# Layer-norm statistics and a check flag sent through DRAM, ScalarE copying all five sums, and a planner with other costs, latencies and due times

## The chip, the core and the metric

The kernel runs on one core of a Trainium2 chip. The metric is the device time of one execution in microseconds (us); lower is better. A time given for a kernel is the median of its runs. The core's engines each take their own queue of instructions in order: TensorE (PE) does the matmuls and transposes, VectorE (DVE) and ScalarE (ACT) the elementwise work, GpSimd (POOL) a few small operations and the DMAs that add into memory, SyncE (SP) issues most DMAs. An instruction waits where it stands until its semaphores allow it, and everything behind it on that engine waits too.

## The reference

One sequence of 2048 tokens with 640 features goes through a layer norm. A state-space convolution (S4D) and a two-layer network with the Mish activation both read the normalised input, and their results are added to the input.

```
xn = _layernorm(x)
...
dt = jnp.exp(log_dt)
A = -jnp.exp(log_A_real) + 1j * A_imag
C = (C_real + 1j * C_imag) * dt[:, None]
P = jnp.exp((A * dt[:, None])[:, :, None] * pos[None, None, :])
K = 2.0 * jnp.einsum("dn,dnl->dl", C, P).real
y = irfft(rfft(u_t, L2) * rfft(K, L2)[None], L2)[:, :, :L]
... y + u * D_skip
h = jnp.einsum("bsd,df->bsf", x, w1) + b1
act = h * jnp.tanh(softplus(h))
return jnp.einsum("bsf,fd->bsd", act, w2)
...
return x + _A_ref(xn, ...) + _B_ref(xn, ...)
```

The sizes are L = 2048, D = 640, N = 128 states for each feature and F = 1728 hidden units, all in float32.

## The kernel before

**Tiles.** Tokens go in four blocks of 512 (`TB`), features in five chunks of 128 (`KD`), hidden units in 14 chunks (`NF`): 13 of 128 and one of 64, chunk 8. Everything on chip is held transposed, features on partitions and tokens along the row. Each float32 operand of a matmul is split into a float16 hi part and a float16 lo part (what the hi part leaves), and a product is hi x hi + hi x lo + lo x hi. ACT makes the hi parts with a scaled copy, DVE the lo parts with one scalar_tensor_tensor: `hi_w1`/`lo_w1` and `hi_w2`/`lo_w2` for the weights, `hi0`/`lo0` for block 0 of the input and `hi_x`/`lo_x` for the others. Weights stay on chip once split.

**Network.** For every block and hidden chunk the first product (`mm1`, and `mm1_pair` for two chunks of the later blocks at once, in a form that needs fewer multiplications: parts one, two, three_a, three_b, four, with sums of weights and of inputs made ahead) fills a PSUM bank. Then a chain of ACT and DVE steps makes Mish: `sig` (sg), `mul` (v1), `mish_a1` to `mish_a3` (arctan, square, tanh), `mish_v3`, `mish_a4` (hi) and `mish_v4` (lo). The second product (`mm2_ops`, `mm2_last`) adds chunk after chunk into the five PSUM banks `ACC`, three chunks behind the first product (`LAG`). At the end of a block the five sums leave `ACC` by `join`: banks 0 and 1 by DVE, banks 2 to 4 by ACT. GpSimd's DMAs add the input to them, and `finish` and `store` add them to the block and store it.

**Recurrence.** The state-space part is done by two scans on DVE for each block and feature chunk (`skip_a` to `skip_e`), with coefficients worked out from the parameters (`mode_ops`). This form, and the scaling of the float16 splits, are right for parameters and weights within certain bounds. So the kernel measures them: `chk` squares and sums the weights, `chk_end` gives each partition a factor `ok`, `ok_sum` adds the 128 factors with a matmul by `ones`, `ok_end` makes a flag of the sum, and `load_flag` reads it into a register. A general form of the computation behind an If runs where the flag is set; with these inputs it isn't.

**Layer norm.** Block 0 is normalised at the start (`stat_ops`, `moments`, `norm0`, `norm0_a`), token by token, and then transposed by PE (`to_t0`) into `ACC`, from where ACT's `hi0` copies make `xh` and DVE's `lo0` make `xl`. For blocks 1 to 3 `stats` takes mean and variance of each token (DVE), `rstds` makes the pair (mean, 1/deviation) in a tile `st_row` of 128 x 8 (POOL), `spread` transposes that tile on PE into eight rows, `spread_a` copies the rows out of PSUM (ACT), `spread_d` writes them to DRAM, `spread_l` loads each row spread over all 128 partitions (`bc`), and `norm_t` applies them to the transposed input.

**What sets the order.** The program has two parts, each emitted under `tc.manual_schedule()`. The first, the start-up, is a string `ORDER`: S and M are statistics, N and A normalisation on DVE and ACT, T the transposes, H and L the hi and lo copies of a w1 chunk, h and l those of block 0's input (one feature chunk, one half of the tokens), and strings such as `0hhlh4a` products of the first three hidden chunks. Ahead of it stand the loads, all on SyncE's queue (half of the first two input tiles on ACT's):

```
for i in range(2):
    load_w1(i)
    sp.dma_start(X0[:, i + 2], xr[0, i + 2])
load_w1(2)
sp.dma_start(cv[:, 0:24], vec)
load_w1(3); load_w2(0); load_w1(4); load_w2(1); load_w1(5)
fill(13)
```

`fill` issues 13 small matmuls that warm PE up. The second part is all the rest, given as operations to a planner (`Plan`): `whole` adds each with its engine, a cost, what must be over before it (`pre`), the buffers that it takes and drops, and sometimes a due time; `run` simulates the engines with these costs, a gap behind each operation (`GAP`) and a latency behind each load, and emits the operations in the order in which that simulation starts them. PE's operations keep the order in which they are added. For the other engines the due time decides among those that could start: `dues` works it out backward from PE's order. The planner starts its engines at given times (`Plan({...})`), and takes the weights of the start-up as loaded: `("hw2", f)` for f = 0 and 1 and `("hw1", f)` for f = 4 and 5 have no load among what they wait for in the plan. These are ACT's hi copies of w2 chunks 0 and 1 and of w1 chunks 4 and 5. The real waits, on semaphores, are put in from the tiles that an instruction reads and writes.

Of the kernel before, what the change touches and what calls it, by code (L numbers as in the profile page):

```python
# [20 lines left out]
P = 128  # L21
# [37 lines left out]

class Plan:  # L60


    GAP = {"PE": 0.22, "ACT": 0.12, "DVE": 0.12, "SP": 0.0, "POOL": 0.3}
# [23 lines left out]
    def add(self, name, eng, cost, fn, pre=(), take=None, drop=(), due=None, rel=0.0, kb=0.0):  # L87
        assert name not in self.ops, name
        self.ops[name] = o = dict(name=name, eng=eng, cost=cost, fn=fn, pre=[p for p in pre if p not in self.end],
                                  take=take, drop=drop, due=1e9, soft=1e9 if due is None else due, rel=rel, kb=kb, n=len(self.ops))  # L90
        if eng == "PE":
            self.pe.append(o)
# [14 lines left out]
    def dues(self):  # L107
# [22 lines left out]
        for o in reversed(order):  # L130
            for p in o["pre"]:
                q = self.ops[p]
                if q["eng"] != "PE":
                    wait = 4.0 if q["kb"] else self.GAP[q["eng"]]
                    for u in ("due", "soft"):
                        q[u] = min(q[u], o[u] - o["cost"] - wait)

    def run(self):
        self.dues()
        todo = {e: {} for e in self.t}  # L140
# [3 lines left out]
        while any(todo.values()):  # L144
# [308 lines left out]
def body(ctx: ExitStack, tc: tile.TileContext, x, xT, logA, Aim, Cr, Ci, logdt, vec, w1, w1T, w2, w2T, out):  # L453
# [29 lines left out]
    ones = cst.tile([P, P], F32, name="ones")  # L483
    g.memset(ones, 1.0)
# [35 lines left out]
    pl = Plan({"PE": 20.05, "ACT": 15.5, "DVE": 17.0, "SP": 15.0, "POOL": 15.0})  # L520
# [115 lines left out]
    def spread():  # L636

        pe.transpose(TR[:2 * NT, 0:P], NX["st"].rearrange("p j i -> p (j i)"), ident)

    def spread_a():  # L640
        NX["sr"] = tmp.tile([2 * NT, P], F32, name="sr")
        a.copy(NX["sr"], TR[:2 * NT, 0:P])

    def spread_d():
        NX["sd"] = dram.tile([2 * NT, P], F32, name="sd")
        sp.dma_start(NX["sd"], NX["sr"])
# [17 lines left out]
    def mode_ops():  # L664
# [6 lines left out]
        yield "ACT", 3.4, lambda: a.activation(t()[:, 0], t()[:, 0], AF.Exp)  # L671
# [3 lines left out]
        for k in range(KD):  # L675
            yield "ACT", 0.5, lambda k=k: a.activation(t()[:, 2, k], t()[:, 2, k], AF.Copy, accum_out=sm[:, 0, k:k + 1])
# [53 lines left out]
    def ok_sum():  # L730
        pe.matmul(TR[:, 0:1], ones, SM["ok"], start=True, stop=True)
# [4 lines left out]
    def ok_end():  # L736
        v.tensor_scalar(flag, TR[0:1, 0:1], P - 0.5, None, op0=OP.is_lt)
# [27 lines left out]
    def join(b, k):  # L765
        r = pl["r", b, k]
        if k < 2:
            v.tensor_scalar(r, ACC[k], 1 / SO, None, op0=OP.mult)  # L768
        else:
            a.activation(r, ACC[k], AF.Copy, scale=1 / SO)  # L770
# [165 lines left out]
    def whole():  # L936
# [9 lines left out]
        def chain(b, f, pre, drop=()):  # L946
# [3 lines left out]
            if b > 0 and f in PAIRS:  # L950
                add(("sX", *n), A, 0.36, sig, b, f, PX, CA, pre=[("two", *n)], take=("s", ("s", *n), 2))
                add(("vX", *n), V, 0.38, mul, b, f, PX, CA, pre=[("sX", *n)], take=("A", ("A", *n), 1))
                add(("sg", *n), A, 0.36, sig, b, f, PZ, CB, pre=[("three_b", *n), ("sX", *n)])
                add(("v1", *n), V, 0.38, mul, b, f, PZ, CB, pre=[("sg", *n), ("vX", *n)], drop=[("s", *n)])
            else:
                add(("sg", *n), A, t(0.60, 0.36), sig, b, f, pre=pre, take=("s", ("s", *n), 2))
                add(("v1", *n), V, t(0.68, 0.38), mul, b, f, pre=[("sg", *n)], take=("A", ("A", *n), 1), drop=[("s", *n)])
            add(("a1", *n), A, t(0.63, 0.36), mish_a1, b, f, pre=[("sg", *n)], take=("p", ("p", *n), 1), drop=[("s", *n)])
            add(("a2", *n), A, t(0.63, 0.36), mish_a2, b, f, pre=[("a1", *n)])
            add(("a3", *n), A, t(0.63, 0.36), mish_a3, b, f, pre=[("a2", *n)])  # L960
            add(("v3", *n), V, t(0.61, 0.36), mish_v3, b, f, pre=[("a3", *n), ("v1", *n)], drop=[("p", *n)])
            add(("a4", *n), A, t(0.54, 1.44), mish_a4, b, f, pre=[("v3", *n)], take=("h", ("h", *n), 1))
            add(("v4", *n), V, t(0.62, 0.80), mish_v4, b, f, pre=[("a4", *n)], drop=[("A", *n)])
# [23 lines left out]
        for f in range(3):  # L987
            pl.end["m1", 0, f] = (16.7, 17.95, 20.1)[f]


        for f in range(NF):
            if f > 5:
                add(("lw1", f), S, 0.1, load_w1, f, take=("w", ("w1", f), 1), kb=327.0)
            if f > 3:
                add(("hw1", f), A, 0.65, hi_w1, f, pre=[("lw1", f)] if f > 5 else [])
                add(("ow1", f), V, 0.75, lo_w1, f, pre=[("hw1", f)], drop=[("w1", f)])
# [3 lines left out]
            add(("ow2", f), V, 0.75, lo_w2, f, pre=[("hw2", f)], drop=[("w2", f)])  # L1000
        for f in range(3):
            chain(0, f, [("m1", 0, f)])
        for f in range(3, NF):
# [4 lines left out]
            if f == 7:  # L1008
                add(("spread", 1), M, 0.1, spread, pre=[("rs", 1)])
# [7 lines left out]
        for b in range(1, NB):  # L1017
            for f in range(NF):
# [20 lines left out]
                lastA = [("v1", 0, 2), ("sr", 1)] if first else [("cY", *p0), ("vX", *p0)]  # L1039
                if (b, i) in ((1, 4), (2, 4), (3, 4)) and b < NB - 1:  # L1040
                    lastA.append(("sr", b + 1))
                if (b, i) == (NB - 1, NP - 1):
                    lastA.append(("oke",))
# [5 lines left out]
                add(("cV", *n), A, 0.36, lambda: a.copy(PVS, PV), pre=[("one", *n)] + ([] if first else [("w", *p0)]))  # L1049
                add(("cY", *n), A, 0.36, lambda: a.copy(PY, PX), pre=[("cV", *n), lastC])  # L1050
                A2[0]()
                add(("two", *n), M, 15 * M2, two, pre=[("cY", *n)] + SWD(1) + TXD(1) + XLD((1, 3, 4)))
                add(("z", *n), V, 0.38, lambda: v.tensor_tensor(PZ, PY, PVS, op=OP.add), pre=[("two", *n), lastB])
# [3 lines left out]
                add(("w", *n), V, 0.38, lambda: v.tensor_tensor(PW, PY, PVS, op=OP.add), pre=[("three_a", *n)])  # L1057
                add(("three_b", *n), M, 9 * M2, three_b, pre=[("z", *n)])
                if i == 3 and b < NB - 1:
                    add(("spread", b + 1), M, 0.1, spread, pre=[("rs", b + 1), ("vX", *n)])  # L1060
                if i == NP - 2 and b == NB - 1:
                    add(("oks",), M, 0.1, ok_sum, pre=[("ce", "last"), ("vX", *n)])
                    add(("oke",), V, 0.17, ok_end, pre=[("oks",)])
# [38 lines left out]
        for c in range(1, NB):  # L1102
            b = c - 1
            t0 = start(b, 0)
            for i in range(NT):
                add(("lx", c, i), S, 0.1, lambda c=c, i=i: sp.dma_start(pl["x", c, i], xr[c, i]),
                    pre=[("st", c, i - 2)] if i > 1 else [], take=("x", ("x", c, i), 1), rel=t0, kb=327.0)
                add(("st", c, i), V, 1.1, stats, c, i, pre=[("lx", c, i)] + [("st", c, i - 1)] * (i > 0), drop=[("x", c, i)])
            add(("rs", c), G, 2.6, rstds, pre=[("st", c, NT - 1)])
            add(("sr", c), A, 0.25, spread_a, pre=[("spread", c)])  # L1110
# [3 lines left out]
            add(("lxt", c), S, 0.5, load_xt, c, pre=old, rel=t0 + 10, kb=1310.0)  # L1114
# [233 lines left out]
```

## Time and profile before

| | |
|---|---|
| median of three runs | 357.91 us (357.82 to 358.10) |
| profiled execution, span of its trace | 356.0 us |
| VectorE busy | 305.9 us (86%) |
| ScalarE busy | 295.8 us (83%) |
| GpSimd busy | 48.9 us (14%) |
| moved by DMA | 48.75 MB, 137 GB/s on average |
| instructions | 6197 |

The profile is of one execution. Its page gives the busy time of each engine, the span in 40 slices, the DMA queues, the chain of work that ended last, and the costliest groups of instructions; the trace behind it tells each instruction's start and length. A row such as `7.86 1.21 ACT L1239 ACTIVATE xh<-acc 128x256 ... x4 [0.34 <-PE acc L1236]` reads: at 7.86 us from the span's start, over 1.21 us, ACT ran four instructions of line 1239 that read `acc` and write `xh`, and before them stood idle for 0.34 us, which the transposes of line 1236 on PE ended. `SPq` and `POOLq` are the queues on which SyncE and GpSimd issue DMAs. A helper's line covers all its calls, so operations are told apart by their tiles.

### The profile page before, as it was taken

Reading aid. Unit: us, or ns where it says so; the run is one execution under the profiler, and the core shown is the slowest. Engines: PE = TensorE matmul, PEld = TensorE weight load, DVE = VectorE, ACT = ScalarE, POOL = GpSimd, SP = SyncE. Lnnn points to the kernel's source line nnn. Section 1 sums busy time; section 2 is a strip of 40 time slices with the busy share of each in tenths; the row PEclk is TensorE's granted clock in tenths of the full one; section 3 lists DMA queues with packets and bytes.
Section 4 is the critical chain, followed back from the end, with each engine's and each line's share of the span. In section 5 each row is a group of like instructions: output and inputs, shape, how many; then the busy total and the mean of one; then the engine's idle time right before and its main releaser. Section 6 shows DMA issues by size and latency. Waiting matters only on the chain.

```text
span 356.0 us, 6197 instructions
## 1 busy us (share of the span) xinstructions
PE 350.0 (98%) x2257; PEld 215.1 (60%) x2257; DVE 305.9 (86%) x583; ACT 295.8 (83%) x620; POOL 48.9 (14%) x74
## 2 busy tenths in 40 slices
PE   7999999999999999999999999999999999999996
PEld 6754444444666666665566666566566666666543
DVE  5989989989999999999999877899988878895552
ACT  4699999987598699989899977989989979877650
POOL 2200010000014221000004341000002443000000
PEclk9999999999999999999999999999999999999999
DMA  7869964402819926910445982931000994032004
GB/s 266 327 175 288 321 217 121 142 0 66 287 56 159 295 71 142 347 40 3 130 151 88 252 204 77 309 120 40 28 0 7 164 216 102 18 58 32 2 2 152
DMA packets 26052, 48.75 MB, mean 137 GB/s; under 512 B 3592, under 2 KB 6944, under 8 KB 26016
## 3 DMA queue, kind: packets, MB, share of 16 engines
q1 hardware_dynamic: 19488, 34.86, 30.0%
q0 software_dynamic: 6240, 13.11, 18.5%
q8 instruction: 19, 0.31, 0.4%
q10 hardware_dynamic: 288, 0.33, 0.3%
q14 instruction: 17, 0.14, 0.2%
HBM read 39.10 MB, written 5.26 MB: 125 GB/s over the span
## 4 chain that ended last, share of the span: by engine, by line
PE 96%; DVE 1%; DMA 1%; ACT 0%; issue 0%
PE acc L859 48%; PE h L827 18%; PE h L807 12%; PE tr L827 12%; PE h L800 2%; PE h L789 2%; PE tr L789 1%; DMA x<-in_A_u_dram 1%; PE acc L1236 0%; DVE st L627 0%; DVE st L628 0%; ACT x L1224 0%; PE acc L873 0%; PE acc L871 0%; PE acc L870 0%; DVE w1l L556 0%
## 5 line engine op out<-in xcount | busy, mean ns | idle before, releaser
L859 PE MATMUL acc<-hi,w2h 128*128 128x512 f16 x273 | 100.9, 379 | 0.0
L859 PE MATMUL acc<-hi,w2l 128*128 128x512 f16 (+1 forms) x265 | 99.7, 379 | 0.0
L859 PE MATMUL acc<-lo,w2h 128*128 128x512 f16 x253 | 93.3, 379 | 0.0
L859 PEld LDWEIGHTS <-w2h 128*128 128x128 f16 x526 | 50.9, 98 | 48.3 <-issue 2.1
L890 ACT ACTIVATE s<-h,cv 128x512 f32<-128x512 f32 (+1 forms) x55 | 32.7, 595 | 28.6 <-PE h L827 23.4
L827 PEld LDWEIGHTS <-w1h 128*128 128x128 f16 x432 | 42.3, 98 | 10.7
L910 DVE SCALAR_TENSOR_TENSOR A<-p,A 128x512 f32<-128x512 f32 (+1 forms) x56 | 37.1, 662 | 8.5 <-ACT p L906 8.2
L859 PEld LDWEIGHTS <-w2l 128*128 128x128 f16 x273 | 25.6, 98 | 30.7 <-issue 1.1
L926 DVE SCALAR_TENSOR_TENSOR lo<-A,hi 128x512 f16<-128x512 f32 x52 | 35.5, 683 | 8.0 <-ACT hi L916 8.0
L894 DVE SCALAR_TENSOR_TENSOR A<-h,bs,s 128x512 f32<-128x512 f32 (+1 forms) x55 | 34.9, 637 | 6.2 <-ACT s L890 6.2
L898 ACT ACTIVATE p<-s,kc 128x512 f32<-128x512 f32 (+1 forms) x56 | 39.4, 703 | 0.6
L902 ACT ACTIVATE p<-p,kc 128x512 f32<-128x512 f32 (+1 forms) x56 | 39.4, 703 | 0.5
L906 ACT ACTIVATE p<-p,kc 128x512 f32<-128x512 f32 (+1 forms) x56 | 39.3, 702 | 0.4
L916 ACT ACTIVATE hi<-A 128x512 f16<-128x512 f32 x52 | 32.5, 626 | 2.6 <-DVE A L910 2.5
L548 POOL DMA_DIRECT2D r<-in_xT_dram x15 | 13.4, 1003 | 131.7 <-DVE r L768 66.3
L749 DVE TENSOR_TENSOR_SCAN g<-g,car,kc 128x512 f32<-128x512 f32 x20 | 25.6, 1278 | 1.7 <-ACT g L743 1.7
L827 PEld LDWEIGHTS <-w1l 128*128 128x128 f16 x216 | 21.1, 98 | 8.2
L753 DVE TENSOR_TENSOR_SCAN g<-g,car,g 128x512 f32<-128x512 f32 x20 | 25.5, 1276 | 0.0
L827 PE MATMUL tr<-xh,w1l 128*128 128x256 f16 x90 | 24.5, 273 | 0.0
L827 PE MATMUL tr<-xh,w1h 128*128 128x256 f16 x90 | 24.5, 273 | 0.0
L827 PE MATMUL tr<-xl,w1h 128*128 128x256 f16 x90 | 24.5, 273 | 0.0
L827 PEld LDWEIGHTS <-swh 128*128 128x128 f16 x216 | 21.1, 98 | 4.4
(177 smaller groups left out, 726.6 us busy)
## 6 DMA issues: line engine op xcount, KB each, us to landing
w<-in_w_dram SPq DMA_DIRECT2D x25, 320.0 KB, 4.9
x<-in_A_u_dram SPq DMA_DIRECT2D x14, 320.0 KB, 5.0
w<-in_w2T_dram SPq DMA_DIRECT2D x15, 288.0 KB, 6.4
w<-in_B_w_dram SPq DMA_DIRECT2D x13, 320.0 KB, 3.4
w<-in_w1T_dram SPq DMA_DIRECT2D x13, 320.0 KB, 7.0
xt<-in_xT_dram SPq DMA_DIRECT2D x15, 256.0 KB, 5.6
r<-in_xT_dram POOLq DMA_DIRECT2D x15, 256.0 KB, 5.6
xt<-r POOLq DMA_DIRECT2D x15, 256.0 KB, 4.6
```

The lines of the kernel that those rows point to most:

```text
L749: v.tensor_tensor_scan(g1[:, 1:], g1[:, 1:], zero.to_broadcast([P, TB]), car[:, 1, k:k + 1], op0=OP.add, op1=OP.add)
L807: pe.matmul(o, w, x, start=(j == 0), stop=(j == len(order) - 1))
L827: pe.matmul(o, p, q, start=start and n == 1, stop=n == 3 * len(w), skip_group_check=True)
L859: pe.matmul(o, w, x, start=start, stop=stop)
L890: a.activation(pl["s", b, f][:, c], bank(b, f)[:, c] if h is None else h, AF.Sigmoid, bias=cv[:, f:f + 1], scale=1 / SH)
L894: v.scalar_tensor_tensor(pl["A", b, f][:, c], bank(b, f)[:, c] if h is None else h, bs[:, f:f + 1], pl["s", b, f][:, c], op0=OP.add, op1=O ...
L898: a.activation(pl["p", b, f][:, cols(f)], pl["s", b, f][:, cols(f)], AF.Arctan, bias=one, scale=-1.0)
L902: a.activation(p, p, AF.Square, bias=pi4, scale=2.0)
L906: a.activation(p, p, AF.Tanh, bias=mb, scale=MG)
L910: v.scalar_tensor_tensor(A, pl["p", b, f][:, cols(f)], MC, A, op0=OP.add, op1=OP.mult)
L916: a.activation(hi, A, AF.Copy, scale=MA * SA / SH)
L926: v.scalar_tensor_tensor(lo, A, MA * SA / SH, hi, op0=OP.mult, op1=OP.subtract)
```

## The change

1. *Statistics.* `spread` and `spread_a` go. `spread_d` writes `st_row` straight to DRAM, turned by the access pattern of the DMA: 1024 single words of 4 bytes, where before eight rows of 512 bytes were written. `spread_l` is as before.
2. *Flag.* `ok_sum`, `ones` and the matmul go. `ok_row` writes the 128 factors to DRAM, `ok_back` loads them into one partition, and `ok_end` takes their minimum on DVE and makes the flag of it.
3. *Sums.* `join` has ACT copy all five banks of `ACC`.
4. *The planner's numbers.* Each operation gets the latency of its load as an argument (`lat`), PE's and ACT's gaps change, most costs change, the start times change by 0.3 to 0.35 us, and an operation can't be taken as ready before work of the start-up that it depends on.
5. *Due times.* A table `SHIFT` of 194 entries moves the due time of single operations, by their number in the plan, by -30 to 30 us, after `dues` has worked them out.

The first product's parts no longer wait in the plan for the copy of the rows (`sr`) or the flag's end (`oke`), since `TR` isn't used for them. The order of PE's operations in `whole` is the same, without the transposes and the ones. The core of the diff:

```
+SHIFT = [e.split(":") for e in (
+    "2:16.5 4:-11 5:-7.5 8:22.5 9:7.5 12:29 21:-23.5 27:12.5 28:-28 29:30 37:-23.5 39:5.5 40:22 41:19.5 45:16 "
...
+    "1335:-18.5 1336:-3.5 ").split()]
...
-    GAP = {"PE": 0.22, "ACT": 0.12, "DVE": 0.12, "SP": 0.0, "POOL": 0.3}
+    GAP = {"PE": 0.17, "ACT": 0.14, "DVE": 0.12, "SP": 0.0, "POOL": 0.3}
...
-    def add(self, name, eng, cost, fn, pre=(), take=None, drop=(), due=None, rel=0.0, kb=0.0):
+    def add(self, name, eng, cost, fn, pre=(), take=None, drop=(), due=None, rel=0.0, kb=0.0, lat=1.9):
         assert name not in self.ops, name
+        rel = max([rel] + [self.end[p] for p in pre if p in self.end])
...
-                    wait = 4.0 if q["kb"] else self.GAP[q["eng"]]
+                    wait = q["lat"] + 2.1 if q["kb"] else self.GAP[q["eng"]]
...
     def run(self):
         self.dues()
+        ops = list(self.ops.values())
+        for i, x in SHIFT:
+            for u in ("due", "soft"):
+                ops[int(i)][u] += float(x)
...
-                end = max(end, self.dma + 1.9)
+                end = max(end, self.dma + o["lat"])
...
-    pl = Plan({"PE": 20.05, "ACT": 15.5, "DVE": 17.0, "SP": 15.0, "POOL": 15.0})
+    pl = Plan({"PE": 20.4, "ACT": 15.8, "DVE": 17.3, "SP": 15.0, "POOL": 15.0})
...
-    def spread():
-
-        pe.transpose(TR[:2 * NT, 0:P], NX["st"].rearrange("p j i -> p (j i)"), ident)
-
-    def spread_a():
-        NX["sr"] = tmp.tile([2 * NT, P], F32, name="sr")
-        a.copy(NX["sr"], TR[:2 * NT, 0:P])
-
     def spread_d():
         NX["sd"] = dram.tile([2 * NT, P], F32, name="sd")
-        sp.dma_start(NX["sd"], NX["sr"])
+        sp.dma_start(NX["sd"].rearrange("r p -> p r"), NX["st"].rearrange("p j i -> p (j i)"))
...
-    def ok_sum():
-        pe.matmul(TR[:, 0:1], ones, SM["ok"], start=True, stop=True)
+    def ok_row():
+        NX["ok"] = tmp.tile([1, P], F32, name="ok_row")
+        z = dram.tile([P], F32, name="ok_dram", bufs=1)
+        sp.dma_start(z.rearrange("(p o) -> p o", o=1), SM["ok"])
+        NX["okd"] = z
+
+    def ok_back():
+        sp.dma_start(NX["ok"], NX["okd"].rearrange("(o p) -> o p", o=1))
...
     def ok_end():
-        v.tensor_scalar(flag, TR[0:1, 0:1], P - 0.5, None, op0=OP.is_lt)
+        z = tmp.tile([1, 1], F32, name="ok_all")
+        yield lambda: v.tensor_reduce(z, NX["ok"], axis=AX.X, op=OP.min)
+        yield lambda: v.tensor_scalar(flag, z, 0.5, None, op0=OP.is_lt)
...
         r = pl["r", b, k]
-        if k < 2:
-            v.tensor_scalar(r, ACC[k], 1 / SO, None, op0=OP.mult)
-        else:
-            a.activation(r, ACC[k], AF.Copy, scale=1 / SO)
+        a.activation(r, ACC[k], AF.Copy, scale=1 / SO)
...
-                add(("sg", *n), A, t(0.60, 0.36), sig, b, f, pre=pre, take=("s", ("s", *n), 2))
...
+                add(("sg", *n), A, t(0.575, 0.357), sig, b, f, pre=pre, take=("s", ("s", *n), 2))
...
-            pl.end["m1", 0, f] = (16.7, 17.95, 20.1)[f]
+            pl.end["m1", 0, f] = (17.0, 18.25, 20.55)[f]
...
-                add(("hw1", f), A, 0.65, hi_w1, f, pre=[("lw1", f)] if f > 5 else [])
...
+                add(("hw1", f), A, 0.628, hi_w1, f, pre=[("lw1", f)] if f > 5 else [])
...
-            add(("hw2", f), A, 0.65, hi_w2, f, pre=[("lw2", f)] if f > 1 else [])
...
+            add(("hw2", f), A, 0.628, hi_w2, f, pre=[("lw2", f)] if f > 1 else [])
...
-            if f == 7:
-                add(("spread", 1), M, 0.1, spread, pre=[("rs", 1)])
...
-                    add(("oks",), M, 0.1, ok_sum, pre=[("ce", "last"), ("vX", *n)])
-                    add(("oke",), V, 0.17, ok_end, pre=[("oks",)])
...
-            add(("sd", c), S, 0.1, spread_d, pre=[("sr", c)], kb=4.0)
-            add(("bc", c), S, 0.2, spread_l, c, pre=[("sd", c)], take=("b", ("b", c), 2 * KD), kb=512.0)
+            add(("sd", c), S, 0.1, spread_d, pre=[("rs", c)], kb=4.0, lat=10.0)
+            add(("bc", c), S, 0.2, spread_l, c, pre=[("sd", c)], take=("b", ("b", c), 2 * KD), kb=512.0, lat=3.0)
...
+        add(("okd",), S, 0.1, ok_row, pre=last, kb=1.0, lat=8.0)
+        add(("okr",), S, 0.1, ok_back, pre=[("okd",)], kb=1.0, lat=8.0)
+        fns = list(ok_end())
+        add(("oke", 0), V, 0.2, fns[0], pre=[("okr",)])
+        add(("oke",), V, 0.17, fns[1], pre=[("oke", 0)])
```

The order of the built instructions differs on ACT, DVE, SP and POOL. Three places follow; the numbers at the end of a tile's name are those that the compiler gives and differ between the two kernels.

**ACT at the start.** In the kernel before, the start-up on ACT runs from the first normalisation (`x`) over the hi copies of w1 chunk 0 (`w1h_113`) and of the input (`xh`), with the copies of w1 chunks 1 to 3 between them, as `ORDER` has it:

```order
L1283 ACTIVATE kc<-kc 128x1
L1224 ACTIVATE x_257<-x_257,rs_259 128x640
L552 ACTIVATE w1h_113<-w_219 128x640
L1239 ACTIVATE xh_172<-acc_216 128x256
L1239 ACTIVATE xh_168<-acc_214 128x256
L1239 ACTIVATE xh_169<-acc_214 128x256
L1239 ACTIVATE xh_170<-acc_215 128x256
L552 ACTIVATE w1h_114<-w_221 128x640
```

Its end, with the first rows of the plan behind it (`bs` is the start-up's last; `w2h_140` is the hi part of w2 chunk 0, `w1h_117` that of w1 chunk 4, `s` the sigmoid, `p` the steps behind it):

```order
L1309 ACTIVATE bs<-cv 128x14
L890 ACTIVATE s_242<-h_211,cv 128x512
L559 ACTIVATE w2h_140<-w_220 128x640
L898 ACTIVATE p_247<-s_242,kc 128x512
L890 ACTIVATE s_243<-h_212,cv 128x512
L902 ACTIVATE p_247<-p_247,kc 128x512
L552 ACTIVATE w1h_117<-w_225 128x640
```

In the changed kernel the same start reads as follows (`w1h_111` is w1 chunk 0, `w2h_138` w2 chunk 0, `w1h_115` w1 chunk 4):

```order
L1297 ACTIVATE kc<-kc 128x1
L1238 ACTIVATE x_255<-x_255,rs_257 128x640
L576 ACTIVATE w1h_111<-w_217 128x640
L583 ACTIVATE w2h_138<-w_218 128x640
L576 ACTIVATE w1h_115<-w_223 128x640
L1253 ACTIVATE xh_170<-acc_214 128x256
L1253 ACTIVATE xh_166<-acc_212 128x256
L1253 ACTIVATE xh_167<-acc_212 128x256
L1253 ACTIVATE xh_168<-acc_213 128x256
L576 ACTIVATE w1h_112<-w_219 128x640
```

The copies of w2 chunk 0 and w1 chunk 4 stood behind the plan's first sigmoid; now they stand between the copy of w1 chunk 0 and the first copy of the input.

**PE at the first transpose of statistics.** The end of a first product (`h`) in block 0 and the second product (`acc`) behind it, before:

```order
L807 LDWEIGHTS w1l_134
L807 MATMUL h_211<-xh_172,w1l_134 128x512
L638 MATMUL tr<-ident,st_row 8x128
L859 LDWEIGHTS w2h_144
L859 MATMUL acc_214<-hi_249,w2h_144 128x512
```

and now:

```order
L828 LDWEIGHTS w1l_132
L828 MATMUL h_209<-xh_170,w1l_132 128x512
L880 LDWEIGHTS w2h_142
L880 MATMUL acc_212<-hi_249,w2h_142 128x512
L880 LDWEIGHTS w2h_142
```

The transpose of `st_row` is gone, and nothing else moved there.

**ACT at the end of block 0.** The sums leaving `ACC` (`r<-acc`), with the steps of block 1's first pair (`pvs`, the copy `h<-tr`, `s`) among them. Before, with the sums of banks 2, 3 and 4:

```order
L1049 COPY pvs<-tr 128x256
L906 ACTIVATE p_248<-p_248,kc 128x512
L1050 COPY h_212<-tr 128x256
L916 ACTIVATE hi_253<-A_244 128x512
L770 ACTIVATE r_236<-acc_216 128x512
L598 ACTIVATE swh_189<-t_231 128x512
L890 ACTIVATE s_243<-tr,cv 128x256
L770 ACTIVATE r_238<-acc_217 128x512
L770 ACTIVATE r_239<-acc_218 128x512
```

and now, with banks 2, 1, 0 and 3 of the five:

```order
L1064 COPY pvs<-tr 128x256
L622 ACTIVATE swh_187<-t_227 128x512
L1065 COPY h_210<-tr 128x256
L937 ACTIVATE hi_251<-A_243 128x512
L791 ACTIVATE r_233<-acc_214 128x512
L791 ACTIVATE r_234<-acc_213 128x512
L927 ACTIVATE p_246<-p_246,kc 128x512
L622 ACTIVATE w1h_116<-t_229 128x2x128
L791 ACTIVATE r_235<-acc_212 128x512
L911 ACTIVATE s_241<-tr,cv 128x256
L791 ACTIVATE r_236<-acc_215 128x512
```

The sums of banks 0 and 1, which DVE made before, stand among ACT's, ahead of the sigmoid of the pair.

More of the change, by code (lines that the diff above doesn't have):

```diff
@@ L958, in chain @@
[L958 to L962, printed above, removed]
@@ new lines, in chain @@
+            add(("a1", *n), A, t(0.614, 0.41), mish_a1, b, f, pre=[("sg", *n)], take=("p", ("p", *n), 1), drop=[("s", *n)])
+            add(("a2", *n), A, t(0.614, 0.41), mish_a2, b, f, pre=[("a1", *n)])
+            add(("a3", *n), A, t(0.614, 0.41), mish_a3, b, f, pre=[("a2", *n)])
+            add(("v3", *n), V, t(0.602, 0.34), mish_v3, b, f, pre=[("a3", *n), ("v1", *n)], drop=[("p", *n)])
+            add(("a4", *n), A, t(0.522, 1.35), mish_a4, b, f, pre=[("v3", *n)], take=("h", ("h", *n), 1))
@@ L965, in second @@
+            add(("v4", *n), V, t(0.602, 0.75), mish_v4, b, f, pre=[("a4", *n)], drop=[("A", *n)])
         def second(b, f, parts):
@@ L1038, in whole @@
                 lastC = ("v1", 0, LAST - 1) if first else ("v1", p0[0], p0[1] + 1)
[L1039 to L1043, printed above, removed]
+                lastA = [("v1", 0, 2)] if first else [("cY", *p0), ("vX", *p0)]
                 SWD = lambda j: [("os", i, j)] if b == 1 else []
```

73 lines of the change are left out of this document (33 added, 40 removed), and 14 rows, old and new, of the table SHIFT.

## The prediction

> **What bounds the kernel now.** I read the page first, then the table by stretches, then the waits of TensorE (PE), then the start in order of time. Parts 1 and 4 of the page:
>
> ```profile
> PE 350.0 (98%) x2257; PEld 215.1 (60%) x2257; DVE 305.9 (86%) x583; ACT 295.8 (83%) x620; POOL 48.9 (14%) x74
> ...
> PE 96%; DVE 1%; DMA 1%; ACT 0%; issue 0%
> ```
>
> PE is busy for 98% of the span and carries 96% of the chain that ended last. "Busy" can hide stalls inside pipelined matmuls, so the next views are the table by stretches (its columns: stretch, length, then busy time and count of PE, PEld, DVE, ACT, POOL, then granted clock, DMA share, GB/s) and PE's own waits:
>
> ```profile
> 20.00:352.00 332.00, 332.00 (x2122) 199.95 (x2120) 290.93 (x543) 283.86 (x597) 44.72 (x59) 1.00 0.48 128
> ```
>
> ```profile
> PE tr L1246 <- POOL ident masks.py:199: 1.5, 1, 1.5
> PE acc L1236 <- ACT x L1224: 1.0, 1, 1.0
> ```
>
> From 20 to 352 us PE has no gap: 332.00 of 332.00. Its only two listed waits lie before 7 us. Two things follow. No better plan can make the middle shorter, except by taking work off PE. And whatever delays PE in the first 20 us is added to the end in full, since nothing later has slack to give it back. So the change is decided by PE's removed instructions and by the start.
>
> The start, in order of time: ACT's rows, then PE's (start, length, what ran, and in brackets the idle time before it).
>
> ```profile
> 6.80 0.72 ACT L552 ACTIVATE w1h<-w 128x640 f16<-128x640 f32 x1
> 7.86 1.21 ACT L1239 ACTIVATE xh<-acc 128x256 f16<-128x256 f32 x4 [0.34 <-PE acc L1236]
> 8.93 0.76 ACT L552 ACTIVATE w1h<-w 128x640 f16<-128x640 f32 x1
> 9.56 0.40 ACT L1239 ACTIVATE xh<-acc 128x256 f16<-128x256 f32 x1
> ...
> 16.99 0.69 ACT L890 ACTIVATE s<-h,cv 128x512 f32<-128x512 f32 x1 [1.27 <-PE h L789]
> 17.58 0.73 ACT L559 ACTIVATE w2h<-w 128x640 f16<-128x640 f32 x1
> ```
>
> ```profile
> 6.95 1.31 PE L1236 MATMUL acc<-ident,x 128*128 128x128 f32 x10 [0.98 <-ACT x L1224]
> 8.29 0.27 PE L789 MATMUL h<-xh,w1h 128*128 128x256 f16 x1
> ...
> 11.96 0.71 PE L1236 MATMUL acc<-ident,x 128*128 128x128 f32 x5
> ...
> 13.27 0.27 PE L789 MATMUL tr<-xl,w1h 128*128 128x256 f16 x1
> 13.56 0.76 PE L1236 MATMUL acc<-ident,x 128*128 128x128 f32 x5
> ```
>
> The first product of the first layer (8.29) starts 0.43 us behind the first xh copy (7.86). That copy is PE's feed.
>
> **Term 1: what PE loses.** Three transposes for the statistics and the matmul with ones go.
>
> ```profile
> 49.31 0.27 PE L638 MATMUL tr<-ident,st_row 128*8 128x128 f32 x1
> 49.42 0.38 PE L859 MATMUL acc<-hi,w2h 128*128 128x512 f16 x1
> ...
> 321.43 0.28 PE L731 MATMUL tr<-ok,ones 128*128 128x1 f32 x2
> 321.57 0.38 PE L859 MATMUL acc<-hi,w2h 128*128 128x512 f16 x1
> ```
>
> From start to next start they take 0.11 and 0.14 us. 3 x 0.11 + 0.14 = **0.47 us less**, all on the path.
>
> **Term 2: two weight copies get in front of the first xh copy.** This is not in the diff; the order of ACT's queue shows it. The plan now begins with the hi copies of w2 chunk 0 and w1 chunk 4, which wait for nothing but their loads. They stand in the built queue not behind the start-up part but inside it, between the first w1h copy (6.80) and the first xh copy (7.86). Before, the plan began with the sigmoid, which waits for PE (16.99), and both copies came after it. An engine takes its queue in order, so the xh copies now wait for two loads:
>
> ```profile
> 5.61 0.49 SPq L543 DMA_DIRECT2D w<-in_B_w_dram  x1
> 6.15 0.43 SPq L538 DMA_DIRECT2D w<-in_w_dram  x1
> ```
>
> ```profile
> w<-in_w_dram SPq DMA_DIRECT2D x1, 320.0 KB, 5.8
> ```
>
> The second fence is the DMA view of just that stretch: w1 chunk 4 lands 5.8 us behind its issue at 6.15, so at 11.95. The w2 load is issued earlier, at 5.61, and its landing isn't told; I take it as landed first. Then the w1 copy starts at about 12.0 (0.05 us to get going), and a copy of this form holds ACT for 0.63 us until the next instruction (8.93 to 9.56). The first xh copy starts at 11.95 + 0.05 + 0.63 = 12.63 instead of 7.86: **4.77 us later**. If the w2 load landed only just with the other, the copies run one behind the other and it is 0.63 us more: 5.40. That is the upper end of this term.
>
> What is queued behind on ACT: the other xh copies, the next w1h copies, the second normalisation, and with them all of PE's products and VectorE's (DVE) xl differences, in unchanged order. One old stall goes: PE's transposes at 13.56 could have run at 13.27 + 0.11 = 13.38 and waited for DVE:
>
> ```profile
> 9.10 0.41 DVE L1242 SCALAR_TENSOR_TENSOR xl<-acc,xh 128x256 f16<-128x256 f32 x1
> ...
> 12.89 0.61 DVE L1221 TENSOR_SCALAR x<-x,mv,rs 128x640 f32<-128x640 f32 x1
> ```
>
> DVE needs 12.89 + 0.61 - 9.10 = 4.40 us from its first xl to that tile. Its first xl can now start at 12.63 + 0.39 + 0.03 = 13.05 (0.39 us is one xh copy), so the tile is there at 17.45, while PE comes at 13.38 + 4.77 = 18.15. The stall of 0.18 us is gone: 4.77 - 0.18 = **4.59 us more**.
>
> **Term 3: PE's clock.** PE's transposes end at 6.95 + 1.31 = 8.26 and its first product now starts at 12.63 + 0.43 = 13.06: 4.8 us without work. Two places of this trace tell what that may do:
>
> ```profile
> 1.47:4.30 2.83, 2.83 (x13) 2.83 (x14) 0.72 (x2) 1.49 (x2) 0.04 (x2) 1.00 0.90 276
> 4.30:5.97 1.67, 1.67 (x15) 1.48 (x14) 1.53 (x6) 0.00 (x0) 0.84 (x2) 1.00 0.88 261
> ...
> 8.29:11.96 3.67, 3.61 (x30) 2.66 (x30) 3.57 (x13) 3.42 (x8) 0.99 (x3) 1.00 1.04 405
> 352.58:355.87 3.29, 0.01 (x1) 0.00 (x0) 0.42 (x1) 0.00 (x0) 0.00 (x0) 1.00 0.37 126
> 355.87:356.04 0.17, 0.00 (x0) 0.00 (x0) 0.00 (x0) 0.00 (x0) 0.00 (x0) 0.51 0.00 0
> ```
>
> Equal warm-up matmuls take 2.83/13 = 0.22 us each up to 4.30 and 1.67/15 = 0.11 behind it, so PE starts at half speed and needs 2.83 us of work to leave it (the clock column still says 1.00 there). At the end it drops to 0.51 after 3.29 us without a matmul. 4.8 us is longer than 3.29, so I take it that PE resumes at half speed and needs those 2.83 us again. In 8.29 to 11.96 it issues 29 products of 0.11 us, 3.16 us of work in 3.67; the 0.51 us of stalls between them absorb part. The loss is 2.83/2 - 0.51 = **0.90 us**. Bounds: 0 (the clock holds) and about (2.83 + 3.29)/2 - 0.51 = 2.55 (it takes a further such stretch).
>
> The Trainium skill ("TensorE: Matmul & The Clock Gate", Part 1: The HAM clock gate) says the array falls to half its clock after an idle window of about 3.4 us and is released after a busy one of about 3.4 us; both ends of this trace agree in kind (3.29 and 2.83 us). By that page's figure the loss would be an estimated 3.4/2 - 0.51 = 1.2 us, so 363.2 instead of 362.9.
>
> **Edits that I cost at nothing.** *Five sums on ScalarE (ACT).* ACT gets six more sums:
>
> ```profile
> 104.66 0.60 ACT L770 ACTIVATE r<-acc 128x512 f32<-128x512 f32 x1
> ...
> 106.94 1.25 ACT L770 ACTIVATE r<-acc 128x512 f32<-128x512 f32 x2 [0.80 <-PE acc L859]
> ```
>
> ```profile
> 107.39 0.38 PE L859 MATMUL acc<-hi,w2h 128*128 128x512 f16 x1
> ```
>
> In old times: three sums can start at 104.66; in the new order the sum of bank 0 is third, with two sums (0.49 each until the next starts), a tanh (0.61) and a small copy (0.31) ahead, and takes 0.60: 104.66 + 0.98 + 0.92 + 0.60 = 107.16, against PE's first overwrite at 107.39. 0.23 us of cover, so nothing; once that is used up, each later microsecond is PE's. *Statistics and flag through DRAM.* The transfer of single words is not in the trace. The nearest, eight rows of 512 B, let the next issue on SyncE go on after 1.25 us:
>
> ```profile
> 220.19 0.29 SPq L646 DMA_DIRECT2D sd<-sr  x1
> 221.44 0.91 SPq L650 DMA_DIRECT2D bc<-sd  x2
> ...
> L654 DVE TENSOR_TENSOR xt<-xt,bc x30: 665/684/692, 65.1 to 251.0; 128x512 f32<-128x512 f32 x30
> L633 POOL TENSOR_SCALAR st_row<-mv x3: 249/367/468, 44.1 to 210.7; 128x4 f32<-128x4 f32 x3
> ```
>
> Statistics are made at 44.1 and first used at 65.1, some 20 us, so even ten times 1.25 us stays covered. It could only gain by nothing, since PE never waits there. The flag's last factor is written at 314.2 and PE reads the flag at 330.7: 16.5 us for two small transfers. *The new order elsewhere.* It can't gain (332.00 of 332.00) and may lose a few tenths where a feeder now stands later; I take 0 and keep 1.0 for the range (about four losses of the size of that 0.23 us cover).
>
> **Sum.** The profiled execution has a span of 356.05 and lies 1.86 us below the median of 357.91; I keep those 1.86. -0.47 + 4.59 + 0.90 = +5.02, so 361.07 of span and **362.9 us**.
>
> **Rivals.**
> - *The clock holds.* Same delay, no half speed: 357.91 - 0.47 + 4.59 = **362.0**. For it: a single drop after 3.29 us doesn't say that every gap of 4.8 us is enough. The same section of the Trainium skill calls the window free-running, by which a gap of 4.8 us need not contain a whole one; this trace fits that, with one drop in it. Chance 0.30.
> - *More is lost at the start or in the middle.* The w2 load lands late (+0.63), the half speed lasts longer (up to 2.55 in place of 0.90), or a feeder is late at some block (up to 1.0): 363.6 to 365.5. Chance 0.14.
> - *Not slower: the hold is not there.* One mechanism: the two loads are down before ACT gets to the copies. It decides at ACT's idle place: both copies must be over by 7.86, where ACT is free from 7.43 at the earliest, so the loads would have to land some 5 us before 11.95. Then only term 1 is left: **357.4**, within 0.2%. Against it: the order of the loads on SyncE ahead of these copies is the same. Chance 0.05.
> - *Faster by more than 0.2%* (0.72 us; about what a measurement of this kernel can tell from no change) needs more than PE's 0.47. Chance 0.01.
>
> **Numbers.** The forecast, 362.4 to 363.6, has 0.50. With the rival 362.0 and the near end of the third case, 361.8 to 363.9 holds about 0.8. Faster 0.01, within 0.2% 0.05, slower 0.94.
>
> **What would show it.** ACT: after the first w1h copy an idle gap of about 4.4 us ended by a load, then a w2h and a w1h copy, then xh at about 12.6. PE: idle from 8.3 to about 13.1, matmuls 0.22 us apart for 2 to 3 us behind it (or 0.11 at once, the first rival), the first full-width first-layer block at about 25.7 instead of 20.2. Behind that PE without gaps and without the rows of the transposes and the ones. I'm wrong if the xh copies start near 7.9, or if PE waits after 26 us.

## The result and the profile after

The changed kernel takes **380.62 us** (median of five runs, 379.33 to 381.21) against 358.01 us (357.82 to 358.20) for the kernel before on the same chip: a ratio of 1.0624 (95% interval 1.0607 to 1.0640). The forecast was 362.9 us, in 361.8 to 363.9. The sign was right; 17.7 of the 22.6 us lost were not foreseen. The profiled execution took 379.33 us, with a span of 376.7. One run of experiment 9 (1329.82 us) and one of the kernel before beside it (2112.61 us) were in a far slower state and are left out.

Parts 1 and 4 of its page, then PE's waits (total, times, longest):

```profile
PE 356.4 (95%) x2252; PEld 218.9 (58%) x2252; DVE 302.1 (80%) x578; ACT 299.7 (80%) x623; POOL 50.0 (13%) x73
...
PE 68%; DMA 12%; DVE 10%; ACT 6%; issue 2%; POOL 0%; SPq 0%; DVEq 0%; POOLq 0%
```

```profile
PE tr L848 <- ACT h L1065: 10.1, 3, 5.3
PE h L810 <- ACT xh L1253: 5.0, 1, 5.0
```

PE's share of the chain fell from 96% to 68%, and 12% now are DMAs. PE's wait for `xh` is the one at the start that was forecast. The three waits for the copy `h<-tr` of a pair were not.

**The start.** ACT's rows and PE's:

```profile
11.56 0.74 ACT L583 ACTIVATE w2h<-w 128x640 f16<-128x640 f32 x1 [4.05 <-DMA w<-in_B_w_dram]
12.39 0.74 ACT L576 ACTIVATE w1h<-w 128x640 f16<-128x640 f32 x1
13.03 1.19 ACT L1253 ACTIVATE xh<-acc 128x256 f16<-128x256 f32 x4
```

```profile
13.45 0.37 PE L810 MATMUL h<-xh,w1h 128*128 128x256 f16 x1 [5.02 <-ACT xh L1253]
13.62 0.42 PE L810 MATMUL h<-xh,w1l 128*128 128x256 f16 x1
13.83 0.42 PE L810 MATMUL h<-xh,w1h 128*128 128x256 f16 x1
```

The two weight copies wait for their loads where the order said they would, the first xh copy starts at 13.03 (forecast 12.63), and products then run 0.21 us apart. The 0.4 us more are the w1 load: in the chain it is issued at 6.22 and lands 6.15 us later, at 12.37, where 11.95 was forecast. The chain in order of time has the first full-width product at 20.34 before and at 26.71 now: 6.37 us lost.

**The middle.** What ACT did around 150 us, and SyncE's queue ahead of it:

```profile
149.29 0.71 ACT L927 ACTIVATE p<-p,kc 128x512 f32<-128x512 f32 x1
155.89 0.74 ACT L722 ACTIVATE w<-w 128x640 f32<-128x640 f32 x1 [5.89 <-DMA w<-in_w1T_dram]
```

```profile
142.84 0.38 SPq L662 DMA_DIRECT2D sd<-st_row  x1
143.26 1.05 SPq L713 DMA_DIRECT2D w<-in_w1T_dram  x2
152.87 0.80 SPq L666 DMA_DIRECT2D bc<-sd  x2
```

Line 662 is the write of 1024 words, and line 713 a load for the weight check, issued 0.42 us behind it. That load landed 12.6 us after its issue. ACT's square of the check (L722) stood for it 5.89 us, and the copy for PE's pair stood behind the square. The stall at 229 us has the same shape: two loads issued at 219.23, behind the third write, landed after 12.4 us (median), and a square waited for one of them:

```profile
ACT w L725 <- DMA w<-in_w2T_dram: 4.9, 1, 4.9
```

The table by stretches (columns as in the prediction):

```profile
13.40:17.30 3.90, 3.85 (x19) 2.66 (x19) 3.13 (x10) 3.77 (x8) 1.23 (x3) 0.50 0.06 25
...
145.00:153.00 8.00, 8.00 (x67) 4.82 (x65) 6.79 (x11) 4.97 (x10) 0.00 (x0) 1.00 0.67 27
153.00:166.00 13.00, 7.70 (x36) 4.26 (x35) 5.70 (x9) 8.26 (x23) 0.94 (x1) 0.74 0.97 272
...
228.00:241.00 13.00, 9.16 (x53) 5.72 (x52) 5.18 (x8) 7.67 (x17) 1.10 (x2) 0.87 0.95 333
```

The row 145 to 153 is the one to learn from: the DMA engines are busy for 0.67 of it and move 27 GB/s. In 153 to 166 PE is idle for 13.00 - 7.70 = 5.30 us, and at half clock behind that:

```profile
159.50:163.00 3.50, 3.47 (x16) 2.31 (x16) 0.86 (x4) 3.48 (x11) 0.87 (x1) 0.50 1.04 320
163.00:166.00 3.00, 3.00 (x15) 1.47 (x14) 3.00 (x4) 1.17 (x4) 0.00 (x0) 0.79 1.06 311
232.80:236.00 3.20, 3.15 (x16) 2.19 (x16) 0.46 (x1) 3.17 (x8) 0.54 (x1) 0.51 1.03 371
```

| where | us |
|---|---|
| start: first full-width product later | 6.4 |
| one short wait at 98 us | 0.9 |
| 153 to 166: idle 5.30, half clock 3.5 x 0.50 + 3.0 x 0.21 | 7.7 |
| 228 to 241: idle 3.84, half clock 3.2 x 0.49 | 5.4 |
| PE's four removed instructions | -0.5 |
| behind PE's last product (6.5 us; before 5.3) | 1.1 |
| sum (measured: 379.33 - 357.91 = 21.4) | 21.0 |

### The profile page after: what moved, and what is told of

The parts are those of the page before. It is cut to its first block, busy times and chain, and to the rows that moved or that the text cites. A ratio compares the mean times of both kernels' runs of the same rounds, so it can differ in the third digit from the quotient of the medians.

```text
span 376.7 us, 6202 instructions
## 1 busy us (share of the span) xinstructions
PE 356.4 (95%) x2252; PEld 218.9 (58%) x2252; DVE 302.1 (80%) x578; ACT 299.7 (80%) x623; POOL 50.0 (13%) x73
## 4 chain that ended last, share of the span: by engine, by line
PE 68%; DMA 12%; DVE 10%; ACT 6%; issue 2%; POOL 0%; SPq 0%; DVEq 0%; POOLq 0%
PE acc L880 32%; PE h L848 15%; PE tr L848 10%; DMA w<-in_w_dram 6%; PE h L828 5%; DMA w<-in_w1T_dram 3%; DMA w<-in_w2T_dram 3%; PE h L810 2%; DVE A L931 1%; DVE xt L670 1%; DVE A L915 1%; DVE w1l L580 1%; PE h L821 1%; ACT hi L937 1%; PE tr L810 1%
## 5 line engine op out<-in xcount | busy, mean ns | idle before, releaser
L848 PE MATMUL tr<-xh,w1h 128*128 128x256 f16 x90 | 25.3, 281 | 10.1 <-ACT h L1065 10.1
L848 PE MATMUL tr<-xl,w1h 128*128 128x256 f16 x90 | 25.4, 282 | 0.0
L848 PE MATMUL tr<-xh,w1l 128*128 128x256 f16 x90 | 25.4, 282 | 0.0
```

Source lines behind the costliest of these rows:

```text
L848: pe.matmul(o, p, q, start=start and n == 1, stop=n == 3 * len(w), skip_group_check=True)
```

## The experiments

Two theories stood for the middle. QUEUE: the write of single words holds the DMAs behind it, and PE stands at the end of that line. PLAN: the new order and due times put the squares too tight behind their loads, whatever the statistics do. WAIT, a third, came in for the sixth run.

**1. The two copies back behind the first sigmoids (e1).**

```
+            held = {("hw2", 0): ("sg", 0, 0), ("hw1", 4): ("sg", 0, 1)}
+            if o["name"] not in held:
+                o["fn"]()
+            for n, at in held.items():
+                if o["name"] == at:
+                    self.ops[n]["fn"]()
```

> The changed kernel with one thing moved: the hi copies of w2 chunk 0 and w1 chunk 4 are written behind the plan's first and second sigmoid, as in the kernel before; all else in the changed kernel's order. Theory QUEUE (two causes: these two copies ahead of the first xh copy cost 6.4 us at the start, of which 4.6 delay and 1.8 half clock; the 1024-word writes hold SyncE's DMA queue some 10 us each, the loads behind them land late, ScalarE stands at a square of a check and PE stands with it, some 14 to 16 us): the first xh copy starts near 7.9 again, the middle stalls stay, 380.6 - 6.4 = 374.2 us (373.2 to 375.2). Rival PLAN (the stalls in the middle come from the new order, costs and due times, not from the words): the same here, 374.2. Rival ELSEWHERE (the start is late for another reason): 380.6, unchanged.

Measured: 372.65 us (370.32 to 375.62), ratio 1.0409 (1.0370 to 1.0448). In its profile the first product starts at 8.52, and the three waits for the copy stay, 9.1 us in all. The time lies a little under the 373.2 to 375.2 that QUEUE and PLAN both gave, and far from ELSEWHERE, which falls. The runs lie 5 us apart, so the size of the start is better read from experiments 2 and 3.

**2. Statistics in 256 runs of 16 bytes (e2), and 3. both edits (e3).** Partition p of the x tiles holds token 4p + i, so that the four tokens of a partition lie side by side in DRAM.

```
+        for j in range(2):
+            sp.dma_start(NX["sd"][j * NT:(j + 1) * NT].rearrange("r p -> (r p)")
+                         .rearrange("(p i) -> p i", i=NT), NX["st"][:, j])
...
```

> The changed kernel with the statistics written as 256 runs of 16 bytes (two DMAs of 128 x 4) in place of 1024 single words; the x tiles for the statistics are loaded with token 4p+i in partition p, so that the row order comes out right. Order of all engines else unchanged. QUEUE: the write takes a quarter, 2 to 3 us, loads behind it are late by no more than that, PE's three stalls (98, 154 and 229 us of the changed trace) go: 380.6 - 14.3 to 16.2 = 364.4 to 366.3, up to 369 if a piece of the stall at 154 is left. PLAN: squares still stand tight behind their loads, 379 to 381.

> Both edits of e1_hold_back and e2_rows16 together. QUEUE: nothing is left but PE's four removed instructions, 358.0 - 0.47 = 357.5 (357.3 to 358.3); PE without gaps from 20 us on. PLAN: 373 to 375, as e1_hold_back alone.

Measured: e2 365.55 us (ratio 1.0200, 1.0184 to 1.0216), e3 358.96 us (1.0025, 1.0015 to 1.0035). The stretch behind the write, in e2:

```profile
145.00:153.00 8.00, 8.00 (x66) 4.90 (x65) 7.87 (x13) 7.97 (x19) 0.05 (x1) 1.00 0.97 295
```

295 GB/s in place of 27, and PE works through. The write lands after 2.7 us (median; the 1024 words took 10.4), and 380.62 - 365.55 = 15.1 us are gone with order, costs and due times as they were. PLAN falls. e3 lies above its 357.3 to 358.3. The two copies alone, e2 against e3, cost 365.55 - 358.96 = 6.6 us.

**4. The rows turned by VectorE (e4)**, in 32 x 32 blocks, and written as 32 pieces of 128 bytes; the copies held back as in e1.

```
+        v.transpose(st_out, st_in)
+        for q in range(0, P, 32):
+            sp.dma_start(NX["sd"][:, q:q + 32], st_out[q:q + 2 * NT])
...
```

> As e1_hold_back, and the statistics are turned by VectorE in 32 x 32 blocks, then written as four DMAs of 8 rows of 128 bytes for each block: 32 pieces where the changed kernel has 1024. VectorE does one more instruction for each of three blocks. QUEUE: 357.5 (357.3 to 358.0), the same as e3_hold_rows or a little under it, since the write is over in about 2 us. PLAN: 373 to 375.

Measured: 359.27 us (1.0032, 1.0020 to 1.0044): a second way without single words, here with the loads of the x tiles as they were, and nearly the same result. But e3 and e4 stay 1.5 and 1.8 us above the 357.5 expected, and 1.0 and 1.3 us above the kernel before. PE's last product ends at 353.08 in e3 and at 352.64 in e4, where 352.59 - 0.47 = 352.1 was to be expected; the rest lies behind it. In e4 PE is full again, with five sums on ACT and the flag through DRAM in place:

```profile
24.00:352.00 328.00, 328.00 (x2097) 197.68 (x2096) 284.55 (x537) 283.89 (x594) 45.62 (x59) 1.00 0.48 128
```

**5. The words alone in the kernel before (e5).**

```
         sp.dma_start(NX["sd"], NX["sr"])
+        sp.dma_start(dram.tile([2 * NT, P], F32, name="words").rearrange("r p -> p r"),
+                     NX["st"].rearrange("p j i -> p (j i)"))
```

> The kernel before, unchanged in its order and its statistics, with one DMA more for each of three blocks: the same 1024 single words written from st_row to a DRAM tile that nothing reads, on SyncE's queue right behind the eight rows. It adds the suspected cost alone; no instruction waits for it. QUEUE: the loads behind it land some 10 us later than in the kernel before; squares that stand 1.6 to 2.4 us behind their loads there hold ScalarE up by 6 to 8 us at about 146 and 231 us: 358.0 + 8 to 18 = 366 to 376. PLAN (the old order has room for the words): 357.9 to 359.

Measured: 368.91 us (1.0303, 1.0288 to 1.0319), 11.0 us for three writes that nobody reads, in the old order. The DMA view of the stretch around the second write (KB, us from issue to landing):

```profile
w<-in_w1T_dram SPq DMA_DIRECT2D x1, 320.0 KB, 12.3
xt<-r POOLq DMA_DIRECT2D x1, 256.0 KB, 12.6
sd<-sr SPq DMA_DIRECT2D x1, 4.0 KB
words<-st_row SPq DMA_DIRECT2D x1, 4.0 KB, 9.8
```

GpSimd's transfer (POOLq), on another queue, is as late as SyncE's (the median of its 15 in this run is 5.1 us). So it isn't one queue that is held but something that both share, and QUEUE needs that correction. The Trainium skill ("DMA: Bandwidth & Descriptors", Issuing engines are not separate DMA queues) says that all issuing engines share the same 16 DMA engines; the 12.6 beside the 12.3 agrees.

**6. bc issued by GpSimd (e6), and 7. the words issued by GpSimd (e7).** In e6 `sp` becomes `g` in `spread_l`, in e7 in `spread_d` (as two DMAs of 512 words).

> The changed kernel with the loads of bc issued by GpSimd in place of SyncE, so that SyncE never stands waiting for the write of the words; the write stays on SyncE's queue. QUEUE: the load behind the write is late as before, since it was issued before bc: 378 to 382, no gain. Rival WAIT (what delays is SyncE standing some 10 us at bc until the words have landed, and the loads behind bc that are issued late): the stalls in the middle go, 364 to 368.

> The changed kernel with the 1024 words written by GpSimd (two DMAs of 512) in place of SyncE; bc stays on SyncE and waits for them. QUEUE: loads on SyncE's queue no longer stand behind the words and land 2 to 7 us after their issue; only those issued behind bc are late: 365 to 371. WAIT: SyncE still stands at bc for 10 us: 378 to 382.

Measured: e6 378.39 us (1.0562, 1.0546 to 1.0579), within QUEUE's 378 to 382 and far from WAIT's 364 to 368. e7 385.73 us (1.0762, 1.0743 to 1.0780), slower than the changed kernel; both theories missed it. The two halves ran one behind the other:

```profile
sd<-st_row POOLq DMA_DIRECT2D x2, 2.0 KB, 10.2
```

512 words take as long there as 1024 on SyncE. From 145 to 155 us, under the first half of the second write, the DMA engines show a busy share of only 0.04, so what takes that long on GpSimd's queue stays open. The rows are thus complete some 20 us after they were made, and the stalls move: the wait at 154 is gone, and VectorE waits 7.0 us for `bc` instead.

**8. and 9. Matmuls that keep PE at work at the start (e8, e9)**, on top of e2: an order token behind the first transposes that issues 44 or 20 matmuls of `ident`.

```
-    ORDER = ("S0 M0 S1 M1 A0 H0 N1 T0 T1 L0 h4a ...
+    ORDER = ("S0 M0 S1 M1 A0 H0 N1 T0 T1 F20 L0 h4a ...
+            elif s[0] == "F":
+                fill(int(s[1:]))
```

> e2_rows16 with 44 small matmuls of ident on PE behind the first ten transposes, to keep PE at work from 8.3 to about 13 us while ScalarE waits for its two loads. The first product still starts at 13.5. If half the clock is what the start loses beside the delay, products run 0.11 us apart from the first on and the time falls by 1.8 to 2.0 us from e2_rows16: 363.6 to 363.8 (363.2 to 364.2). If the products are slow at the start for another reason (feeders late), no change: 365.5.

> As e8_rows_fill with 20 matmuls of ident in place of 44 (each took 0.23 us there, so they end near 12.7 us and no longer stand ahead of the first product). If PE's half clock behind the gap is what the start loses beside the delay: products 0.11 us apart from the first on at 13.4, PE's last matmul ends 1.6 to 2.2 us earlier than in e2_rows16 (359.0), at 356.8 to 357.4; time 363.4 to 364.0, or 0.8 to 1.4 less if the end behind the last store is short as in e8_rows_fill. If it isn't the clock: 359.0 and 365.5.

Measured: e8 366.51 us (1.0236, 1.0222 to 1.0250). Each of its 44 matmuls shows as two records of 0.11 us (88 in 9.99 us), so they took 0.23 us each, not 0.11, and stood ahead of the first product until 18.0. It fits neither account and told little beyond that. e9 362.83 us (median of three; 1.0139, 1.0120 to 1.0158), 2.7 below e2. Its start (the 20 matmuls are the 40 records of the first row):

```profile
8.26 4.63 PE L1261 MATMUL tr<-ident 128*128 128x128 f32 x40
13.06 0.27 PE L811 MATMUL h<-xh,w1h 128*128 128x256 f16 x1 [0.16 <-ACT xh L1254]
13.17 0.27 PE L811 MATMUL h<-xh,w1l 128*128 128x256 f16 x1
```

The products run at full speed from the first on, and PE's last one ends at 356.82 where e2's ends at 359.01: 2.19 us, of which 0.5 are the earlier first product (13.06 against 13.56). The clock is worth 1.7 us in e2. The delay without it is 356.82 - 352.59 (the end before) + 0.47 = 4.70 us in e9. In the profiled changed kernel the split is another: its first full-width product is at 26.71 and e9's at 25.03, and 0.39 of these 1.68 us are its later first product (13.45 against 13.06), so there the clock took 1.3 us and the delay 6.37 - 1.3 = 5.1.

**10. e4 with other places for two copies and 16 warm-up matmuls (e10).**

> e4_dve_turn with two edits: the hi copies of w1 chunks 4 and 6 stand behind the first sigmoid and behind the first chunk's hi step, so that the first second product isn't kept waiting 0.35 us at 23.5 us; and 16 warm-up matmuls at the start in place of 13, which end before the first transposes and only make PE's program longer. Accounts: PE's last matmul 0.3 us earlier than in e4_dve_turn (352.64), at 352.3. If the 0.8 us more that all variants of the changed kernel but e8_rows_fill take behind their last instructions hangs on the length of PE's program: 358.0 (357.6 to 358.2), level with the kernel before. If it doesn't: 358.9 (358.6 to 359.1).

Measured: 358.30 us (1.0011, 1.0002 to 1.0020). PE's last product ended at 352.93, not at 352.3; the three extra matmuls had pushed the first transposes from 7.10 to 7.61. Behind the last instructions of the span it took 1.79 us (before 1.86; the changed kernel 2.66). That agrees with the account by PE's program length, but the time itself lies between the ranges of the two accounts (357.6 to 358.2 and 358.6 to 359.1), so this run alone doesn't decide.

**11. The words of e5, 64 bytes apart in DRAM (e11).**

```
+        words = dram.tile([2 * NT, P, 16], F32, name="words")
+        sp.dma_start(words[:, :, 0].rearrange("r p -> p r"), ...)
```

> e5_before_words with the 1024 words written 64 bytes apart in DRAM in place of side by side. If the transfer holds the DMA engines for its number of single words: 366 to 372 us again (e5_before_words: 368.9), the words landing 9 to 10 us behind their issue. If what takes long is that several engines write words of the same stretch of DRAM: landing after 2 to 4 us, 358 to 361.

Measured: 358.32 us (1.0008, 0.9999 to 1.0018). The same 1024 single words, and no loss. Their landing in e5, then in e11 (median of three), and the stretch behind the second write of each:

```profile
words<-st_row SPq DMA_DIRECT2D x3, 4.0 KB, 9.9
```

```profile
words<-st_row SPq DMA_DIRECT2D x3, 4.0 KB, 3.3
```

```profile
142.00:151.00 9.00, 9.00 (x70) 5.30 (x69) 7.80 (x12) 5.44 (x11) 0.00 (x0) 1.00 0.84 48
```

```profile
142.00:151.00 9.00, 9.00 (x60) 5.67 (x59) 8.72 (x20) 8.81 (x23) 1.43 (x2) 1.00 1.05 368
```

48 GB/s against 368. So it is not the number of single words that holds the transfers up, but that they lie side by side. (This was tried in the old order alone, and at one distance.) The Trainium skill ("DMA: Bandwidth & Descriptors", Rules for kernel authors) warns that a last dimension that isn't contiguous becomes one descriptor for each element. The trace agrees for both runs (29172 DMA packets in each, 26052 in the kernel before), but by the count alone both would have been as slow; the measurement decides against it.

**12. The kernel before with VectorE's turn in place of PE's transposes (e12)**, and three matmuls behind PE's last product to keep its program long.

> The kernel before, in its own order, with the statistics turned by VectorE (32 x 32 blocks, as in e4_dve_turn) and written as four DMAs of 8 rows of 128 bytes, in place of three transposes on PE and three copies on ScalarE; the flag and the sums stay as before. Three matmuls of ident stand behind PE's last product, beside the last stores, so that PE's program stays as long as it was. PE loses 3 x 0.11 us: 357.9 - 0.33 = 357.6 (357.4 to 357.9), PE's last product at 352.3. If VectorE's three instructions make a feeder late, 358 or more.

Measured: 358.68 us (1.0021, 1.0012 to 1.0030). PE's last product ended 0.4 us earlier than before, as expected, and the time rose by 0.8 nevertheless. In the profile SyncE took 1.1 us instead of 0.3 to issue the last store, and the end moved with it. Whether the three added matmuls beside it are to blame wasn't tried. No version here beats the kernel before.

## Why the prediction was wrong

- **What bounds the kernel: right.** PE had no slack behind 20 us, so each stall came through to the end: the table above adds up to 21.0 of 21.4. The prediction's own sign of being wrong, PE waiting after 26 us, came true.
- **Term 1, -0.47: right as far as it shows.** In e12 PE's last product ends 0.4 us earlier without the transposes.
- **Term 2, +4.59: right in kind, and in size where the load landed as forecast.** The copies stood where the order showed them and waited for their loads. The delay without the clock is 4.70 in e9, whose second copy starts at 12.00, and 5.1 in the profiled changed kernel, where the w1 load landed 0.4 us later than forecast.
- **Term 3, +0.90: right in kind, too small.** The clock is worth 1.3 us in the profiled changed kernel and 1.7 in e2. It was taken that PE, once back at work, leaves half speed after 2.83 us, as at the start. But the half clock runs from the middle of the pause, and PE had 4.02 us of work under it here and 4.87 in e2 (rows at the end of this document). The figure of the Trainium skill ("TensorE: Matmul & The Clock Gate", Part 1), a busy window of about 3.4 us, would have come nearer (an estimate of 1.2).
- **"Statistics and flag through DRAM", at nothing: the step that failed,** by 15.1 us (e2). "Even ten times 1.25 us stays covered" was right about the time: the write took 10.4. But it compared this with the 20 us until the rows are first used, and asked only who waits for the write. What matters is what runs beside it and who waits for that: loads on both queues, ACT's squares in an in-order queue, behind them the copy for PE. In the trace before, the first load behind the write landed at 139.13 and its square stood at 143.10; the next, issued at 137.70, landed at 144.79 and its square stood at 146.43. The cover there was 4.0 and 1.6 us, not 20.
- **Five sums on ACT, the flag, the new order: near nothing, as forecast.** e4 has all three and a full PE from 24 to 352. Ahead of that its first second product starts 0.35 us late.
- **Not thought of:** 0.8 us behind the span, which the sum took over unchanged (1.86 before, 2.66 after).
- **The rivals.** "The clock holds" fell: the granted clock is 0.50 behind the pause. "More is lost in the middle" was priced at up to 365.5, with a feeder late by up to 1.0 us. The mechanism that came has its place there, but some fifteen times the price, and its range was drawn from ordinary covers rather than from the one transfer whose kind the trace had never shown.

## What to carry to other kernels

Before a small strided store is called hidden, ask what else uses the DMA engines while it is under way, and how close the consumers of those transfers stand behind their landing; the slack of the store's own reader says nothing about that. Write such data in runs (16 bytes were enough here), turned on chip if need be, rather than as single words side by side. And read the built order of an in-order engine around the start: one copy that waits for a load there costs its whole wait, and the clock on top.

## What else the runs showed

- 1024 words of 4 bytes side by side: 9.4 to 10.4 us, with 27 to 48 GB/s for everything beside them. 64 bytes apart: 2.9 to 4.2 us. 256 runs of 16 bytes in two DMAs: medians of 2.7 to 3.0 (e2, e3, e8, e9). The mechanism behind this was not measured.
- PE's pauses of 5.0 us (until 13.45), 5.3 (until 159.53) and 3.8 (until 232.85), and that of e2 (until 13.56), bring half clock, and it starts before PE is back. Three stretches of the changed kernel, then one of e2; the second number of a row is PE's busy time at half clock:

```profile
10.65:17.47 6.82, 4.02 (x20) 2.76 (x20) 3.30 (x11) 5.52 (x11) 1.40 (x3) 0.50 0.44 175
157.42:164.24 6.82, 4.71 (x19) 2.75 (x19) 3.94 (x7) 6.54 (x19) 0.94 (x1) 0.50 1.04 340
232.52:235.92 3.40, 3.06 (x15) 2.14 (x15) 0.69 (x1) 3.37 (x9) 0.54 (x1) 0.50 1.04 361
```

```profile
11.61:18.43 6.82, 4.87 (x24) 3.44 (x24) 4.04 (x12) 5.52 (x11) 1.87 (x3) 0.50 0.31 123
```

  The Trainium skill ("TensorE: Matmul & The Clock Gate", Part 1) gives about 3.4 us for both windows. The trace agrees: the stretches last 3.4 us or twice that. What a pause costs therefore depends on where in such a stretch PE comes back: 3.06 to 4.87 us of its work ran at half clock here.
- VectorE turns a tile of 128 x 32 in 32 x 32 blocks in 0.21 us (e4).
- The end behind the last instruction of the span takes 1.8 to 1.9 us where PE's program is as long as before or longer (e5, e8 to e12), and 2.65 to 3.25 where it is four instructions shorter (the changed kernel, e1, e2, e3, e6, e7); e4 shows 1.07 us of it inside its span, as a last wait on PE alone. e8 and e9 add only matmuls to e2 and bring 3.25 down to 1.8. Why is open.
